# Gated mix of linear attention and a Mish layer: block 0 gives up two feature steps and takes its num products later, block 1 has an order of its own

## Chip, cores and metric

The kernel runs on one core of one Trainium2 chip. The metric is the device time of one execution in microseconds (us); lower is better. TensorE is PE in the profile, its weight loads PEld, VectorE is DVE, ScalarE is ACT, GpSimd is POOL, and SyncE, which issues nearly all DMAs, is SP.

## What is computed

```python
x = A_x                                        # (1, 2048, 512)
g = sigmoid((x * gate_w).sum(-1, keepdims=True))
q, k, v = split(x @ wqkv)                      # 32 heads of 16
pq = q @ w_phi; pk = k @ w_phi                 # per head, 16 x 16
phi = lambda p: concat([softmax(p), softmax(-p)])
kv = phi(pk).T @ v;  z = phi(pk).sum(rows)     # per head
o = (phi(pq) @ kv) / (phi(pq) @ z + 1e-6)
a = o @ wo
h = x @ w1 + b1                                # 512 -> 1376
b = mish(h) @ w2                               # 1376 -> 512
out = g * a + (1 - g) * b
```

All is fp32. Large products are made of three passes: each operand is split into a high part, rounded to the format that TensorE takes, and the rest (names with h and l), and high x high, high x low and low x high are added up.

## The kernel before

**Stage A** goes over the 2048 rows in 8 chunks of 256. It projects k and v, makes the features of k, adds up kv and z over all rows, and writes the projected q (pq) to DRAM (pqd). Weights are loaded and split along the way.

**Stage B** goes over the rows in four blocks of 512 (b = 0 to 3). A block has two threads of work that meet at its end.

- The Mish layer in 11 slices of 128 hidden units (i = 0 to 10). Each slice has `up` (12 matmuls, line 441), `mi` (Mish on ScalarE), `hi` (its high part, ScalarE), `lo` (the rest, GpSimd, line 461), and `down` (12 matmuls, line 465: three for each of the block's four row groups of 128, added up in four PSUM banks).
- The attention in four row groups of 128 (t = 0 to 3). `lq` loads pq. `mx`, `mn`, `d0`, `d1` (VectorE, lines 233 to 242) take the maximum and minimum per head away; `E` (ScalarE) is the exponential; `S`, `rS` (VectorE) the sums and their reciprocals; `T`, `D`, `m`, `de`, `rd`, `sc`, `es` (VectorE, lines 511 to 541 and 257) the denominator and the scaled features; `tr` (line 527) transposes blocks of 32 x 32 into the tile tt. For each half of a block (h = 0 for t = 0 and 1, h = 1 for t = 2 and 3), `mv` (line 546) moves tt into eT by 16 copies that SyncE issues, `nu` (line 552) multiplies eT with kv (16 matmuls, the num products), `oh` (ScalarE) and `ol` (VectorE) split the product into ohl, and `wo` (line 576, 12 matmuls per row group) multiplies it with wo. `ag` (ScalarE) scales by the gate, `fi` (VectorE, line 593) adds the gated Mish part and stores the rows.

Besides, `gr` takes the gate's logits out of one column of the first up product and brings them through DRAM into columns; `ge` and `gg` make the sigmoid of them. `LX`, `XH`, `XL` load and split x for the next block. `@z`, `@kt`, `WL` are leftovers of stage A in block 0.

**The order** is written out by hand. Each engine takes its instructions in the order in which the steps are named in a text: FIRST, STEADY, NEXT and LAST for stage A (lines 39 to 54), BLOCK0 for block 0 and BLOCK for the others (lines 58 to 74). `run` (line 187) calls the steps one after the other, and every instruction is pinned to that order. A name with `+` is the next block's step; a step that has run is not run again. So a block's first two row groups are worked on ahead, in the block before: in block 0, S1 is the first feature step left, since E0, E1 and S0 were made in LAST. In BLOCK0 and BLOCK, row groups 2 and 3 too are begun in the block before, up to their E (`mx2+` to `E3+`).

In `b_ops` (line 437), the down products of slices 0 to 8 are the steps `dn0` to `dn8`; those of slices 9 and 10 go by row group, as `df0` to `df3` of six matmuls each, each followed by its `fi`.

**What makes steps wait.** Tiles come from rings of few buffers. tt and eT have one buffer each: `tr2` and the next block's `tr0` wait until the copies of the half before have read tt, and `mv` waits until the num products before have read eT. PSUM has three banks with the tag "a" (up, the second half of num, every other wo), four for the down sums, and one with the tag "kv" (the first half of num, the other wo): `wo` of an even row group waits until the first half of `ol` has read the num product out of it. The tag "tx" (two buffers) holds T and the loaded x in turns, so `LX0` and `LX1` wait for the `D` of the next block's row groups 0 and 1. ScalarE has the exponential and Mish in different tables, and a change between them is a table load.

Of the kernel before, what the change touches and what calls it, by code (L numbers as in the profile page):

```python
# [30 lines left out]
NF = NFA + NFB  # L31
# [26 lines left out]
BLOCK0 = """  # L58
    up0 mi0 hi0 lo0 gr S1 rS1 mx2 mn2 d02 d12 up1 @z mi1 hi1 lo1 T0 D0 m0 de0 rd0 sc0 es0 tr0 up2 mi2 hi2 lo2 WL0 dn0
    T1 D1 m1 de1 rd1 sc1 es1 tr1 mv0 lq0+ lq1+ mx3 mn3 d03 d13 up3 @kt mi3 hi3 lo3 WL1 dn1  # L60
    up4 mi4 hi4 lo4 dn2 E2 E3 ge S2 T2 rS2 D2 m2 de2 rd2 sc2 es2 tr2 gg up5 mi5 hi5 lo5 dn3 up6 mi6 hi6 lo6 dn4 nu0 oh0 ol0
    S3 T3 rS3 D3 m3 de3 rd3 sc3 es3 tr3 mv1 up7 mi7 hi7 lo7 dn5 mx0+ mn0+ d00+ d10+ mx1+ mn1+ d01+ d11+ lq2+ lq3+
    up8 mi8 hi8 lo8 wo0 ag0 wo1 ag1 E0+ E1+ dn6 S0+ T0+ rS0+ D0+ m0+ de0+ rd0+ sc0+ es0+ tr0+
    up9 mi9 hi9 lo9 dn7 nu1 oh1 ol1 S1+ T1+ rS1+ D1+ LX0 LX1 m1+ de1+ rd1+ sc1+ es1+ tr1+ mv0+ up10 mi10 hi10 lo10 dn8
    mx2+ mn2+ d02+ d12+ mx3+ mn3+ d03+ d13+ XH0+ XL0+ XH1+ XL1+ wo2 ag2 wo3 ag3 E2+ E3+ df0 fi0 df1 fi1 df2 fi2 df3 fi3
"""
BLOCK = """
    up0 mi0 hi0 lo0 gr S2 T2 rS2 D2 m2 de2 rd2 sc2 es2 tr2 up1 mi1 hi1 lo1 up2 mi2 hi2 lo2 dn0 nu0 oh0 ol0
# [1 line left out]
    mx0+ mn0+ d00+ d10+ mx1+ mn1+ d01+ d11+ lq2+ lq3+ up5 mi5 hi5 lo5 dn3 E0+ E1+ ge gg wo0 ag0 wo1 ag1  # L70
    S0+ T0+ rS0+ D0+ m0+ de0+ rd0+ sc0+ es0+ tr0+ up6 mi6 hi6 lo6 dn4 nu1 oh1 ol1 S1+ T1+ rS1+ D1+ LX0 LX1 m1+ de1+ rd1+ sc1+
    es1+ tr1+ mv0+ up7 mi7 hi7 lo7 dn5 mx2+ mn2+ d02+ d12+ mx3+ mn3+ d03+ d13+ up8 mi8 hi8 lo8 dn6 E2+ E3+
    wo2 ag2 wo3 ag3 up9 mi9 hi9 lo9 dn7 up10 mi10 hi10 lo10 dn8 XH0+ XL0+ XH1+ XL1+ df0 fi0 df1 fi1 df2 fi2 df3 fi3
"""


# [1 line left out]
def tile_gated_mix(ctx: ExitStack, tc: tile.TileContext, xT, wv, wkT, wqT, bd, w1a, w1b, b1, w2a, w2b, wo, out):  # L78
# [9 lines left out]
    def mm(*a, **k):  # L88
        return pin(nc.tensor.matmul(*a, **k))  # L89
# [14 lines left out]
    def psum(name, tag, bufs={"a": 3, "dn": 4, "kv": 1}):  # L104
        nm[0] += 1
        return pp.tile([P, 512], F32, name=f"{name}_{nm[0]}", tag=tag, bufs=bufs[tag])
# [77 lines left out]
    def at(key, name, fn):  # L184
        steps.setdefault((key, name), []).append(fn)

    def run(text, key, prev=None, nxt=None):
        for w in text.split():
            k = prev if w.endswith("'") else nxt if w.endswith("+") else key
            for fn in steps.pop((k, w.rstrip("'+")), ()):  # L190
                fn()
# [160 lines left out]
    def w2_tile(f, x):  # L352
        n_, f = ("w2a", f) if f < NFA else ("w2b", f - NFA)
        return W[n_][0][x][:, f * 512 : (f + 1) * 512]
# [48 lines left out]
    B = {}  # L403
# [33 lines left out]
    def b_ops(b):  # L437
        key = ("B", b)
        U, dn, tts, eTs, num, ohl, io = {}, {}, {}, {}, {}, {}, {}

        def up(i):
            f = ORDER[i]
            xh, xl = xb[b]
            ps = psum("up", "a")
            n = 0
            for w, a in ((0, xh), (1, xh), (0, xl)):
                for k in range(KT):
                    mm(ps, w1_tile(f, w, k), a[:, k, :], start=(n == 0), stop=(n == 3 * KT - 1))
                    n += 1
            U[i] = {"ps": ps}  # L450

        def mi(i):
            f = ORDER[i]
            U[i]["a"] = k2("act", "hl")
            act(U[i]["a"], U[i]["ps"], AF.Mish, bias=b1s[:, f : f + 1])

        def hi(i):
            U[i]["h"] = k2("h", "hl", F32R)
            act(U[i]["h"], U[i]["a"])

        def lo(i):
            U[i]["l"] = k2("l", "hl", F32R)
            pin(G_.tensor_sub(U[i]["l"], U[i]["a"], f32(U[i]["h"])))  # L463

        def down(i, t):
            if t not in dn:
                dn[t] = psum("down", "dn")
            f = ORDER[i]
            h, l = [U[i][x][:, t * P : (t + 1) * P] for x in "hl"]
            for n, (a, x) in enumerate(((h, 0), (h, 1), (l, 0))):  # L470
                mm(dn[t], a, w2_tile(f, x), start=(i == 0 and n == 0), stop=(i == NF - 1 and n == 2))

        for i in range(NF):
            at(key, f"up{i}", lambda i=i: up(i))
            at(key, f"mi{i}", lambda i=i: mi(i))
            at(key, f"hi{i}", lambda i=i: hi(i))
            at(key, f"lo{i}", lambda i=i: lo(i))
            for t in range(4):
                at(key, f"dn{i}" if i < NF - 2 else f"df{t}", lambda i=i, t=t: down(i, t))


        cs = slice(4 * b, 4 * b + 4)
# [127 lines left out]
    for b in range(NB):  # L610
        b_ops(b)
# [51 lines left out]
    for c in range(1, NCH):  # L663
        run(STEADY if c < NCH - 2 else NEXT if c < NCH - 1 else LAST, ("A", c), ("A", c - 1), ("B", 0))
    for b in range(NB):
        run(BLOCK if b else BLOCK0, ("B", b), ("B", b - 1), ("B", b + 1))
    assert not steps, list(steps)


# [58 lines left out]
```

## Time and profile before

| what | value |
|---|---|
| runs | 475.44 us median of 3 (474.42 to 475.58) |
| the profiled execution: own time | 475.38 us |
| its span, first to last instruction | 473.6 us |
| busy: TensorE, VectorE, ScalarE, GpSimd | 462.3, 312.4, 194.0, 160.2 us |
| TensorE's mean granted clock | 0.991 of full speed |
| block 0, first up to the end of its last down | 161.46 to 245.02 us |

Times in the trace are microseconds from the span's start. A row of a time line has start, length (merged if xN is above 1), engine, line, operation, the tiles it writes and reads, and in square brackets the idle time just ahead of it on its engine with what ended it. The chain of waits follows the work that ended last back from the end; its rows have start, length and what. Rows of stretches (A:B) have, behind the length, the busy time of PE, PEld, DVE, ACT and POOL with instruction counts, then TensorE's granted clock, the DMA share and GB/s. Many lines are those of helpers: all matmuls have line 89, all ScalarE operations line 109, so tiles tell them apart.

### The profile page before, as it was taken

The page shows a single profiled execution, that of the slowest core. Times are in us where ns is not written, and L with a number is a line of the kernel's source. Part 1 is how long each engine was busy: PE and PEld are TensorE (multiplying, and loading weights), DVE is VectorE, ACT ScalarE, POOL GpSimd, SP SyncE. Part 2 cuts the span into 40 slices and gives each one's busy share as a digit, 9 for nine tenths or more (in the row PEclk, how much of TensorE's full clock was granted, in tenths as well). Part 3 has the DMA queues.
Part 4 walks back from the last instruction along what each step waited for, and adds up shares of the span by engine and source line. Part 5 has one row for each costly group of instructions (what it writes and reads, how often), then busy time and mean ns, then how long its engine had stood idle before and what let it go on. Part 6 is the DMA issues. An engine that isn't in the chain of part 4 may idle for free.

```text
span 473.6 us, 6002 instructions
## 1 busy us (share of the span) xinstructions
PE 462.3 (98%) x2292; PEld 375.4 (79%) x2292; DVE 312.4 (66%) x402; ACT 194.0 (41%) x263; POOL 160.2 (34%) x102
## 2 busy tenths in 40 slices
PE   7999999999999999699999999999999999999996
PEld 6888888888888878578787887887787888787885
DVE  2597648449498999888998967437867818621002
ACT  3544433533415644425455253533344452334221
POOL 3448685675861355211303212123111121321211
PEclk9999999999999999889999999999999999999999
DMA  7621531523514100403434141312041312020002
GB/s 289 222 89 46 177 101 57 174 62 122 181 42 157 44 2 1 124 10 88 133 85 140 36 142 46 88 44 91 2 117 59 101 33 91 1 72 18 0 2 89
DMA packets 25237, 40.01 MB, mean 84 GB/s; under 512 B 5620, under 2 KB 13812, under 8 KB 25208
## 3 DMA queue, kind: packets, MB, share of 16 engines
q1 hardware_dynamic: 25032, 39.35, 27.2%
q8 instruction: 18, 0.29, 0.3%
q10 hardware_dynamic: 144, 0.26, 0.2%
q14 instruction: 11, 0.09, 0.1%
q0 software_dynamic: 32, 0.01, 0.0%
HBM read 22.82 MB, written 8.40 MB: 66 GB/s over the span
## 4 chain that ended last, share of the span: by engine, by line
PE 86%; DVE 8%; SPq 2%; DMA 2%; POOL 1%; issue 1%; ACT 0%; POOLq 0%; DVEq 0%
PE proj L89 26%; PE down L89 22%; PE up L89 22%; PE wo L89 9%; PE num L89 4%; PE kvp L89 2%; SPq L550 2%; DMA wT<-in_wkT_dram 1%; PE fuse L89 1%; DVE E L257 1%; DVE Sm L246 1%; DVE Dn L537 1%; DVE E L240 1%; POOL zacc L295 1%; DVE E L242 1%
## 5 line engine op out<-in xcount | busy, mean ns | idle before, releaser
L463 POOL TENSOR_TENSOR l<-act,h 128x512 fp32r<-128x512 f32 x44 | 59.3, 1349 | 237.2 <-ACT h L109 208.5
L109 ACT ACTIVATE act<-up,b1s 128x512 f32<-128x512 f32 x44 | 30.3, 689 | 97.9 <-PE up L89 97.8
L295 POOL TENSOR_TENSOR zacc<-zacc,E 128x1024 f32<-128x1024 f32 x16 | 39.7, 2480 | 50.5 <-ACT v L109 37.3
L109 ACT ACTIVATE E<-E 128x1024 f32<-128x1024 f32 x32 | 33.5, 1058 | 42.7 <-DVE E L242 42.7
L257 DVE TENSOR_TENSOR E<-E,Sm 128x1024 f32<-128x1024 f32 x32 | 44.0, 1374 | 1.1
L89 PE MATMUL wo<-woh,ohl 128*128 128x512 f32 x128 | 40.7, 389 | 0.0
L246 DVE TENSOR_REDUCE Sm<-E 128x64 f32<-128x1024 f32 x32 | 38.7, 1210 | 2.2 <-ACT E L109 2.2
L89 PE MATMUL down<-w2ah,h 128*128 128x512 f32 x96 | 37.5, 390 | 0.0
L89 PE MATMUL down<-w2ah,l 128*128 128x512 f32 x96 | 37.4, 389 | 0.0
L89 PE MATMUL down<-w2al,h 128*128 128x512 f32 x96 | 37.3, 389 | 0.0
L233 DVE TENSOR_REDUCE mx<-proj 128x32 f32<-128x512 f32 x16 | 11.1, 691 | 37.3 <-PE proj L89 37.3
L595 DVE SCALAR_TENSOR_TENSOR io<-down,og_sb,io 128x512 f32<-128x512 f32 x16 | 11.5, 746 | 31.4 <-PE down L89 31.4
L89 PE MATMUL down<-w2bh,h 128*128 128x512 f32 x80 | 31.1, 389 | 0.0
L89 PE MATMUL down<-w2bl,h 128*128 128x512 f32 x80 | 31.1, 389 | 0.0
L89 PE MATMUL down<-w2bh,l 128*128 128x512 f32 x80 | 31.1, 389 | 0.0
L569 DVE TENSOR_TENSOR ohl<-num,ohl 128x512 fp32r<-128x512 f32 x16 | 10.9, 688 | 27.5 <-ACT ohl L109 27.5
L375 DVE TENSOR_TENSOR xbl<-xraw,xbh 128x1024 fp32r<-128x1024 f32 x8 | 12.2, 1566 | 24.7 <-ACT xbh L109 24.7
L109 ACT ACT_TABLE_LOAD x17 | 21.8, 1283 | 16.2 <-PE up L89 16.0
L109 ACT ACTIVATE h<-act 128x512 fp32r<-128x512 f32 x44 | 27.8, 632 | 1.5
L89 PEld LDWEIGHTS wo<-woh,ohl 128*128 128x128 f32 x128 | 24.0, 188 | 5.0
L89 PE MATMUL up<-xbh,w1ah 128*128 128x512 f32 x96 | 26.3, 396 | 0.2 <-ACT zb L109 0.2
L89 PE MATMUL up<-xbl,w1ah 128*128 128x512 f32 x96 | 25.7, 390 | 0.0
(113 smaller groups left out, 1019.7 us busy)
## 6 DMA issues: line engine op xcount, KB each, us to landing
xraw<-in_xT_dram SPq DMA_DIRECT2D x16, 512.0 KB, 3.5
eT<-tt SPq DMA_DIRECT2D x128, 64.0 KB, 2.0
pqd<-qs SPq DMA_DIRECT2D x16, 256.0 KB, 2.3
pq<-pqd SPq DMA_DIRECT2D x16, 256.0 KB, 2.9
out_dram<-io SPq DMA_DIRECT2D x16, 256.0 KB, 2.0
raw<-in_w1a_dram SPq DMA_DIRECT2D x3, 512.0 KB, 4.6
raw<-in_w2a_dram SPq DMA_DIRECT2D x3, 512.0 KB, 3.7
wT<-in_wkT_dram SPq DMA_DIRECT2D x4, 256.0 KB, 5.7
```

What stands on the lines that cost most here:

```text
L89: return pin(nc.tensor.matmul(*a, **k))
L109: return pin(A_.activation(out_, in_, fn, **k))
L233: pin(V.tensor_reduce(d[name], hv(src()), axis=AX.X, op=op))
L240: pin(V.tensor_sub(E, hv(src()), d["mx"][:, :, None].to_broadcast([P, H, DH])))
L246: pin(V.tensor_reduce(d["S"], hv(d["E"][:, :]), axis=AX.X, op=ALU.add))
L257: pin(eng.tensor_mul(hv(d["E"][:, :]), hv(d["E"][:, :]), d["S"][:, :, None].to_broadcast([P, 2 * H, DH])))
L295: at(key, f"z{t}", lambda d=d: pin(G_.tensor_add(zacc, zacc, d["E"])))
L375: pin(V.tensor_sub(xb[b][1][:, :, sl], kt(raw[h], SC), f32(xb[b][0][:, :, sl])))
L463: pin(G_.tensor_sub(U[i]["l"], U[i]["a"], f32(U[i]["h"])))
L550: pin(Sy.dma_start(eTs[h][32 * k : 32 * k + 32, :, q, :], tts[h][32 * q : 32 * q + 32, :, k, :]))
L569: pin(V.tensor_sub(ohl[h, gp][:, 512:], num[h, gp], f32(ohl[h, gp][:, :512])))
L595: pin(V.scalar_tensor_tensor(io[t], dn[t], og_sb[:, i : i + 1], io[t], op0=ALU.mult, op1=ALU.add))
```

## The change

Only the texts of the order and one name change; every instruction does what it did.

- BLOCK0: E3, ge and gg come later (E2 alone ahead of the slice up5, E3 behind dn3). nu0, oh0 and ol0 come behind up7 and dn5 instead of ahead of up7, with S3, T3, rS3 ahead of ol0. dn6 comes ahead of wo0. up10 and dn8 come ahead of nu1, and S1+, T1+, rS1+, D1+ ahead of ol1. The next block's mx2 to d13, E2 and E3 leave block 0.
- BLOCK1, new, for block 1: it begins with mx2 to d13 and, behind up1, E2 and E3, of its own row groups 2 and 3; up7 and dn5 come ahead of nu1. Else it is as BLOCK.
- In all blocks the down products of slice 9 are one step dn9 ahead of the df steps, which keep slice 10 alone, three matmuls each. In block 0 dn9 stands ahead of wo2, in the others behind dn8 (and XL1+).

```diff
 BLOCK0 = """
     up0 mi0 hi0 lo0 gr S1 rS1 mx2 mn2 d02 d12 up1 @z mi1 hi1 lo1 T0 D0 m0 de0 rd0 sc0 es0 tr0 up2 mi2 hi2 lo2 WL0 dn0
     T1 D1 m1 de1 rd1 sc1 es1 tr1 mv0 lq0+ lq1+ mx3 mn3 d03 d13 up3 @kt mi3 hi3 lo3 WL1 dn1
-    up4 mi4 hi4 lo4 dn2 E2 E3 ge S2 T2 rS2 D2 m2 de2 rd2 sc2 es2 tr2 gg up5 mi5 hi5 lo5 dn3 up6 mi6 hi6 lo6 dn4 nu0 oh0 ol0
-    S3 T3 rS3 D3 m3 de3 rd3 sc3 es3 tr3 mv1 up7 mi7 hi7 lo7 dn5 mx0+ mn0+ d00+ d10+ mx1+ mn1+ d01+ d11+ lq2+ lq3+
-    up8 mi8 hi8 lo8 wo0 ag0 wo1 ag1 E0+ E1+ dn6 S0+ T0+ rS0+ D0+ m0+ de0+ rd0+ sc0+ es0+ tr0+
-    up9 mi9 hi9 lo9 dn7 nu1 oh1 ol1 S1+ T1+ rS1+ D1+ LX0 LX1 m1+ de1+ rd1+ sc1+ es1+ tr1+ mv0+ up10 mi10 hi10 lo10 dn8
-    mx2+ mn2+ d02+ d12+ mx3+ mn3+ d03+ d13+ XH0+ XL0+ XH1+ XL1+ wo2 ag2 wo3 ag3 E2+ E3+ df0 fi0 df1 fi1 df2 fi2 df3 fi3
+    up4 mi4 hi4 lo4 dn2 E2 S2 T2 rS2 D2 m2 de2 rd2 sc2 es2 tr2 up5 mi5 hi5 lo5 dn3 E3 ge gg up6 mi6 hi6 lo6 dn4
+    up7 mi7 hi7 lo7 dn5 nu0 oh0 S3 T3 rS3 ol0 D3 m3 de3 rd3 sc3 es3 tr3 mv1 up8 mi8 hi8 lo8 dn6
+    mx0+ mn0+ d00+ d10+ mx1+ mn1+ d01+ d11+ lq2+ lq3+ wo0 ag0 wo1 ag1 E0+ E1+ S0+ T0+ rS0+ D0+ m0+ de0+ rd0+ sc0+ es0+ tr0+
+    up9 mi9 hi9 lo9 dn7 up10 mi10 hi10 lo10 dn8 S1+ T1+ rS1+ D1+ LX0 LX1 nu1 oh1 ol1 m1+ de1+ rd1+ sc1+ es1+ tr1+ mv0+
+    XH0+ XL0+ XH1+ XL1+ dn9 wo2 ag2 wo3 ag3 df0 fi0 df1 fi1 df2 fi2 df3 fi3
+"""
+BLOCK1 = """
+    up0 mi0 hi0 lo0 gr mx2 mn2 d02 d12 mx3 mn3 d03 d13 up1 mi1 hi1 lo1 E2 E3 S2 T2 rS2 D2 m2 de2 rd2 sc2 es2 tr2
+    up2 mi2 hi2 lo2 dn0 nu0 oh0 ol0 S3 T3 rS3 D3 m3 de3 rd3 sc3 es3 tr3 lq0+ lq1+ mv1 up3 mi3 hi3 lo3 dn1 up4 mi4 hi4 lo4 dn2
+    mx0+ mn0+ d00+ d10+ mx1+ mn1+ d01+ d11+ lq2+ lq3+ up5 mi5 hi5 lo5 dn3 E0+ E1+ ge gg wo0 ag0 wo1 ag1
+    S0+ T0+ rS0+ D0+ m0+ de0+ rd0+ sc0+ es0+ tr0+ up6 mi6 hi6 lo6 dn4 up7 mi7 hi7 lo7 dn5 nu1 oh1 ol1 S1+ T1+ rS1+ D1+ LX0 LX1
+    m1+ de1+ rd1+ sc1+ es1+ tr1+ mv0+ mx2+ mn2+ d02+ d12+ mx3+ mn3+ d03+ d13+ up8 mi8 hi8 lo8 dn6 E2+ E3+
+    wo2 ag2 wo3 ag3 up9 mi9 hi9 lo9 dn7 up10 mi10 hi10 lo10 dn8 XH0+ XL0+ XH1+ XL1+ dn9 df0 fi0 df1 fi1 df2 fi2 df3 fi3
 """
 BLOCK = """
...
-    wo2 ag2 wo3 ag3 up9 mi9 hi9 lo9 dn7 up10 mi10 hi10 lo10 dn8 XH0+ XL0+ XH1+ XL1+ df0 fi0 df1 fi1 df2 fi2 df3 fi3
+    wo2 ag2 wo3 ag3 up9 mi9 hi9 lo9 dn7 up10 mi10 hi10 lo10 dn8 XH0+ XL0+ XH1+ XL1+ dn9 df0 fi0 df1 fi1 df2 fi2 df3 fi3
...
-                at(key, f"dn{i}" if i < NF - 2 else f"df{t}", lambda i=i, t=t: down(i, t))
+                at(key, f"dn{i}" if i < NF - 1 else f"df{t}", lambda i=i, t=t: down(i, t))
...
-        run(BLOCK if b else BLOCK0, ("B", b), ("B", b - 1), ("B", b + 1))
+        run((BLOCK0, BLOCK1, BLOCK, BLOCK)[b], ("B", b), ("B", b - 1), ("B", b + 1))
```

## The prediction, made before the changed kernel had run

> **What bounds the kernel now.** I read the page's first part first, then the mean clock, then the chain of work that ended last, then the time lines of the engines around the one hole that they show.
>
> ```profile
> PE 462.3 (98%) x2292; PEld 375.4 (79%) x2292; DVE 312.4 (66%) x402; ACT 194.0 (41%) x263; POOL 160.2 (34%) x102
> ```
>
> ```profile
> core 0: 473.6 us, clock 0.991
> ```
>
> TensorE (PE) is busy for 462.3 us of a span of 473.6; the program's own time for this execution is 475.38 us, so 1.78 us lie outside the span. 11.3 us of idle TensorE are left, and a busy TensorE isn't always a fast one: a mean clock of 0.991 leaves 0.009 x 473.6 = 4.3 us of lost pulses. So whatever the change does, it can win some 3% at most, and only through holes. The chain of waits, read from 198 us on, shows the one hole inside the run:
>
> ```profile
> 198.11 2.00 DMA eT<-tt
> 200.11 0.04 issue
> 200.15 3.68 PE num L89 x16
> 203.83 3.73 PE up L89 x12
> ...
> 226.59 1.88 PE num L89 x16
> 228.47 2.94 PE up L89 x12
> 231.42 2.72 PE down L89 x12
> 234.14 5.44 PE wo L89 x24
> 239.58 5.44 PE down L89 x24
> ```
>
> The columns are start, length, what. The first num group of block 0 (step nu0) starts when the last copy eT<-tt has landed. It takes 3.68 us, and the up group after it 3.73; the same pair later, in the same block, takes 1.88 and 2.94. The last row, the closing down group of block 0, ends at 245.02: there block 1 starts. The time line of TensorE has the wait, and the stretches of 5 us have the clock:
>
> ```profile
> 200.15 3.68 PE L89 MATMUL num<-eT,kvb 128*64 128x256 f32 x16 [3.75 <-DMA eT<-tt]
> ```
>
> ```profile
> 195.00:200.00 5.00, 1.40 (x7) 0.82 (x5) 3.41 (x4) 0.72 (x2) 2.17 (x2) 0.87 0.43 102
> 200.00:205.00 5.00, 4.85 (x19) 2.76 (x20) 2.76 (x6) 1.19 (x2) 0.00 (x0) 0.50 0.31 104
> ```
>
> TensorE is free from 200.15 - 3.75 = 196.40, and after the wait its granted clock (third figure from the end) is 0.50 over 200 to 205. **The hole's price** is thus the wait, 3.75, and the slow clock, (3.68 - 1.88) + (3.73 - 2.94) = 1.80 + 0.79 = 2.59: together 6.34 us, 1.33% of 475.38.
>
> Why are the copies late? SyncE's time line:
>
> ```profile
> 188.36 10.34 SPq L550 DMA_DIRECT2D eT<-tt  x16
> 198.75 1.09 SPq L509 DMA_DIRECT2D pq<-pqd  x2
> 213.78 10.19 SPq L550 DMA_DIRECT2D eT<-tt  x16
> ```
>
> Sixteen copies take SyncE 10.2 to 10.3 us to issue, and the last lands 2.00 us after its issue. They can't start before tr1, the transpose of the second 128 rows, which ends on VectorE just before 188.36.
>
> **The change, part by part.**
>
> *nu0 behind up7 and dn5.* All steps up to E2 of block 0 stand as before on every engine, so the copies still land at 200.11. TensorE goes on at 196.40 with up7 (2.72) and dn5 (2.72): nu0 comes up at 201.84, 1.73 us after the landing. The wait goes, and with it the slow clock: **-6.34 us**. What is late next must be looked for down block 0. With the chain's prices (up after a num 2.94, a down or num after anything 2.72 or 1.88, wo 2.72 each) TensorE without a wait runs: nu0 201.84, up8 203.72, dn6 206.66, wo0 and wo1 209.38, up9 214.82, dn7 217.54, up10 220.26, dn8 222.98, nu1 225.70, dn9 227.58 (2.94, after a num), wo2 230.52, then wo3 and the four df (2.72 in all), block 1 at 238.68. I walk VectorE against that with these rows:
>
> ```profile
> 200.19 1.25 DVE L531 STREAM_TRANSPOSE tt<-E 128x1024 f32<-128x1024 f32 x1 [1.68 <-DMA eT<-tt]
> ...
> 201.73 0.17 DVE L496 TENSOR_SCALAR og_sb<-g_sb 128x4 f32<-128x4 f32 x1
> ...
> 209.36 1.16 DVE L521 SCALAR_TENSOR_TENSOR den<-Dn 128x32 f32<-128x32 f32 x1
> ...
> 221.57 1.22 DVE L246 TENSOR_REDUCE Sm<-E 128x64 f32<-128x1024 f32 x1 [2.17 <-ACT E L109]
> ...
> 229.06 1.25 DVE L569 TENSOR_TENSOR ohl<-num,ohl 128x512 fp32r<-128x512 f32 x2
> 230.24 1.20 DVE L246 TENSOR_REDUCE Sm<-E 128x64 f32<-128x1024 f32 x1
> ...
> 234.14 0.23 DVE L537 TENSOR_TENSOR Dn<-Dn,Sm 128x64 f32<-128x64 f32 x1
> 234.40 0.19 DVE L521 SCALAR_TENSOR_TENSOR den<-Dn 128x32 f32<-128x32 f32 x1
> ...
> 237.71 0.64 DVE L233 TENSOR_REDUCE mx<-pq 128x32 f32<-128x512 f32 x1
> ```
>
> A feature chain from S to tr lasts 229.06 - 221.57 = 7.49; its first four steps S, T, rS, D 234.14 - 230.24 = 3.90; a pair ol 1.18; mx, mn, d0 and d1 of two row groups are eight steps of at most 0.7, 5.6.
>
> *tr2 and gg* stay where the copies put them: tr2 waits for tt until 200.19 in both, gg ends at 201.90. The new place of lo5 on GpSimd, some 3 us earlier since E3 no longer stands ahead of mi5, may push S2's chain; that chain has 200.19 - 198.51 = 1.68 of idle (in the first row) as cover, so I cost it nothing. *S3, T3, rS3, ol0, D3 to tr3*: 201.90 + 7.49 + 1.18 = 210.57. ol0 is done at about 206, ahead of wo0 at 209.38. The copies mv1 then take 10.19 + 2.00, down at 222.8: nu1, put behind up10 and dn8, comes at 225.70. Margin 2.9.
>
> *The eight steps for block 1's first two row groups* end by 216.2, hidden: S0+ waits for E0+ on ScalarE, which waits for ag1:
>
> ```profile
> 218.47 0.69 ACT L109 ACTIVATE io<-wo,g_sb 128x512 f32<-128x512 f32 x1 [2.03 <-PE wo L89]
> 219.18 1.28 ACT L109 ACT_TABLE_LOAD   x1
> 220.47 2.01 ACT L109 ACTIVATE E<-E 128x1024 f32<-128x1024 f32 x2
> ```
>
> From ag1 at 218.47 to S at 221.57 are 3.10 us; ag1 moves to 214.85, S0+ to 217.95, and tr0+ ends at 225.44 (tt is free at 222.8). *S1+ to D1+ now stand ahead of ol1*: 225.44 + 3.90 = 229.34. The first half of ol1 is done at about 229.95, and wo2 needs it, at 230.52: margin 0.57, **the thinnest of all**. GpSimd can eat it:
>
> ```profile
> 209.14 1.33 POOL L463 TENSOR_TENSOR l<-act,h 128x512 fp32r<-128x512 f32 x1 [11.97 <-ACT h L109]
> ```
>
> While this lo ran, VectorE's den step took 1.16 instead of 0.19 (209.36 against 234.40): 0.97 lost. Two lo (of up9 and up10) fall into 217.95 to 229.34. I take one hit: ol1's half at 230.92, **wo2 waits 0.40**; the bounds are 0 (no hit) and 1.4 (two hits). The Trainium skill has a rule for it, "SBUF — State Buffer", on the shared port pair: a VectorE operation with two SBUF inputs and a GpSimd operation that reads SBUF hold the pair by turns for a whole instruction, and the later one blocks. By it, two hits at the very start of a lo would cost 2 x 1.33 = 2.7 and the wait would be 2.1 (an estimate); the row above, with a finish at 210.52 after a GpSimd end at 210.47, agrees. That is the first rival below.
>
> *Features 2 and 3 of block 1 at that block's head.* XL0+ and XL1+ follow tr1+ directly, which ends at 229.34 + 0.97 + 1.18 + (7.49 - 3.90) = 235.1; two steps as wide as tr2's 1.25, they are done by 237.6, ahead of block 1 (239.08 with the 0.40). The eight steps run behind fi3, to about 246. E2 waits on ScalarE for mi1 and hi1, behind up1's end at 244.5:
>
> ```profile
> L109 ACT ACTIVATE act<-up,b1s 128x512 f32<-128x512 f32 x44 | 30.3, 689 | 97.9 <-PE up L89 97.8
> ```
>
> Two steps of 0.7, a table load of 1.28 and an E of 1.0 put S2 at about 248.5. Its chain, ol0 and S3's chain end near 264.7 (7.49 + 1.18 + 7.49), two pq loads (1.09) and the copies (12.2) are down at 278; nu1 of block 1, put behind up7 and dn5, stands at 249.96 + 1.88 + 2.94 + 11 x 2.72 = 284.7. Margin 6.7: nothing. nu0 of block 1 reads copies that start at 235.1 and land at 247.3; TensorE is there at 249.96 (four groups of 2.72 after 239.08). Margin 2.7: nothing. If either cover were gone, each microsecond behind it costs one. Two more table loads on ScalarE (E3 apart from E2) stand beside TensorE's up and down groups: nothing.
>
> *dn9 ahead of the df steps, in all blocks.* The same twelve matmuls. The last three stores of the run come 0.68 apart instead of 1.36. The stores of block 0, issued half a microsecond apart, and the last four land so (first block 0, then the run's end):
>
> ```profile
> DMA to landing us min/median/max: 2.4/2.5/2.7
> ```
>
> ```profile
> DMA to landing us min/median/max: 2.0/2.0/2.0
> ```
>
> So the end is later by 0 to 0.7; between the two rows I take **+0.3**.
>
> **Sum.** -6.34 + 0.40 + 0.3 = -5.6 against this execution's 475.38: 469.8 us, ahead of the runs' median of 475.44 by 1.2%. Bounds of the terms: -6.34 + 0 + 0 and -6.34 + 2.1 + 0.7, that is 469.0 to 471.8.
>
> **The rivals.**
>
> *ol1 late.* Both lo hit, and wo2 waits 1.4 to 2.1: 475.38 - 6.34 + 1.75 + 0.3 = 471.1. For it: the thin margin, and the row of 1.16. Against: D and S are reductions, and den's neighbours (0.23, 0.19) are short, so a lo has to fall on a small part of the chain. Whether so short a wait also slows the clock is bounded by nothing and by 2.59. On that the Trainium skill, "TensorE: Matmul & The Clock Gate", says that the clock halves after an idle window of about 3.4 us; by it 1.4 to 2.1 us cost themselves alone, and the row of 3.75 with its 0.50 agrees.
>
> *The wait moves to nu1 of block 0.* Its copies need tr3 and 12.2 us of copying. If VectorE ran 6 us behind the walk there, nu1 would wait 3.1 plus up to 2.59 and all would be as before, 475.4. Against: the walk up to tr3 has one lo in it, 0.97 of 2.9.
>
> *Slower, at nu0 of block 1.* The place is the VectorE queue from S0+ to tr1+, behind which its copies stand; SyncE also holds them behind the load LX1, which waits for D1+. The margin is 2.7. A slip of 7.2 us makes a wait of 4.5 plus 2.59, 7.1 against the 5.64 gained: from there the kernel is slower by more than can be measured. With a slip of 8: 475.38 - 5.64 + 5.3 + 2.59 = 477.6. For it: all the margins hang on this one queue, and SyncE issues in order. Against: two lo give 1.9 to 2.7, and no row shown reaches 7.
>
> **How the numbers follow.** Forecast (wo2 waits at most 1 us): 0.76. ol1 late: 0.15. Wait at nu1: 0.03. Slower at block 1: 0.06. A difference under 0.3%, 1.4 us, couldn't be told from none. Faster is forecast and first rival, 0.91; same 0.03; slower 0.06. The range takes the terms' bounds and the runs' own spread (474.42 to 475.58, as much as 1.0 below this execution's time and 0.2 above): 468.4 to 472.0.
>
> **What would show it.** In the changed profile: the num group of block 0 without a wait, 1.88 long, near 201.8; a clock of 1.00 over 200 to 205; block 1's first up near 239 instead of 245.02; the second num near 225.7 without a wait; a wait of up to 1 us for VectorE's ohl ahead of wo2; the rest of the run moved as a whole by some 6 us; the last store landing 2.0 to 2.7 us after its issue. The prediction is wrong if a num group still waits for eT, if wo2 waits over 2 us, or if the clock shows another 0.50.

## The result, and the profile after

The changed kernel takes 470.51 us (median of 4 runs, 469.57 to 470.98) against 475.44 (4 runs, 474.42 to 475.58): a ratio of 0.9898, 95% interval 0.9886 to 0.9909. It is faster by 1.0%; 469.8 was forecast.

The profiled execution took 469.57 us. Its span and mean clock:

```profile
core 0: 467.9 us, clock 1.000
```

The time line of TensorE has no wait at a num group any more; the first one, and the stretches around it, now read:

```profile
201.65 1.95 PE L97 MATMUL num<-eT,kvb 128*64 128x256 f32 x16
```

```profile
195.00:200.00 5.00, 5.00 (x24) 4.14 (x23) 2.16 (x5) 2.13 (x4) 2.02 (x1) 1.00 0.42 100
200.00:205.00 5.00, 5.00 (x30) 3.40 (x29) 4.87 (x8) 1.65 (x3) 1.29 (x1) 1.00 0.32 104
```

(Lines are 8 higher than before: 97 for 89.) TensorE is busy in the whole of both stretches, where it was for 1.40 us of the first, and the clock is 1.00 instead of 0.50 in the second. The only new wait of TensorE stands ahead of wo2 of block 0, for ol1:

```profile
230.74 0.50 PE L97 MATMUL wo<-woh,ohl 128*128 128x512 f32 x1 [0.34 <-DVE ohl L577]
```

In the chain of waits that place and what follows it read:

```profile
230.74 5.74 PE wo L97 x24
236.48 2.72 PE down L97 x12
239.20 8.16 PE up L97 x36
247.36 2.72 PE down L97 x12
250.08 1.88 PE num L97 x16
```

The two wo groups take 5.74 us behind the wait, against 5.44 without one, so ol1 costs 0.34 + 0.30 = 0.64. The 0.30 is no second wait, since TensorE shows no idle time inside the groups. It goes with the restart: without a wait a group begins 0.16 before the one ahead of it has ended (in e5_ol1_earlier below, wo begins at 231.65 and the dn9 ahead of it ends at 231.81), and behind the wait the second matmul starts 0.34 after the first, where 0.23 is usual. Block 1 starts at 239.20 instead of 245.02, and its num products (250.08) don't wait.

**The opening moves.** The profiles differ in when block 0 begins. Two of them, the changed kernel and a later one (e5_again below):

```profile
161.35 1.20 PE L97 MATMUL up<-xbh,w1ah 128*128 128x512 f32 x4
```

```profile
163.55 1.20 PE L97 MATMUL up<-xbh,w1ah 128*128 128x512 f32 x4
```

These 2.2 us come before anything that any of these kernels changes, and the kernel before alone begins block 0 at 161.46, 161.87 and 162.88 in its three profiled executions. So I compare spans from block 0's first up to the end, and name this **the rest**: before 473.6 - 161.46 = 312.1, the changed kernel 467.9 - 161.35 = 306.6 (306.55).

### The profile page after: what moved, and what is told of

The parts are those of the page before. It is cut to its first block, busy times and chain, and to the rows that moved or that the text cites. A ratio compares the mean times of both kernels' runs of the same rounds, so it can differ in the third digit from the quotient of the medians.

```text
span 467.9 us, 6005 instructions
## 1 busy us (share of the span) xinstructions
PE 460.0 (98%) x2292; PEld 374.0 (80%) x2292; DVE 310.6 (66%) x402; ACT 196.4 (42%) x265; POOL 161.7 (35%) x102
## 4 chain that ended last, share of the span: by engine, by line
PE 91%; DVE 3%; SPq 2%; DMA 2%; issue 0%; ACT 0%; DVEq 0%
PE proj L97 28%; PE up L97 24%; PE down L97 23%; PE wo L97 8%; PE kvp L97 3%; PE num L97 3%; SPq L558 2%; DMA wT<-in_wkT_dram 1%; PE fuse L97 1%; DMA pq<-pqd 1%; DVE tt L539 1%; DVE Dn L525 0%; DVE io L603 0%; DVE ohl L577 0%; DVE Sm L533 0%
## 5 line engine op out<-in xcount | busy, mean ns | idle before, releaser
L471 POOL TENSOR_TENSOR l<-act,h 128x512 fp32r<-128x512 f32 x44 | 61.0, 1385 | 229.9 <-ACT h L117 207.0
L97 PE MATMUL up<-xbh,w1al 128*128 128x512 f32 x96 | 25.7, 389 | 0.0
```

## The experiments

Theory: the gain is the hole at nu0, a wait and a slow clock, and the other parts of the change keep new holes from opening behind it. Rivals: that the work taken off VectorE in block 0 is the gain in itself; that nu0's move is all of it; that dn9 is a small cost.

The ratios are to runs of the kernel before that were taken beside each kernel, with medians of 475.44, 475.45, 475.53 and 475.16 us.

| kernel | median us (runs) | ratio to before, 95% | span | first up | rest |
|---|---|---|---|---|---|
| before | 475.44 (4) | | 473.6 | 161.46 | 312.1 |
| changed | 470.51 (4) | 0.9898 (0.9886 to 0.9909) | 467.9 | 161.35 | 306.6 |
| e1_nu0_only | 476.55 (6) | 1.0025 (1.0013 to 1.0037) | 475.8 | 162.30 | 313.5 |
| e2_nu0_back | 476.29 (10) | 1.0015 (1.0005 to 1.0024) | 474.5 | 161.59 | 312.9 |
| e3_nu0_after_up7 | 471.07 (4) | 0.9908 (0.9892 to 0.9925) | 469.2 | 161.61 | 307.6 |
| e4_nu0_half_dn5 | 472.36 (10) | 0.9948 (0.9929 to 0.9966) | 470.6 | 161.62 | 309.0 |
| after_again | 470.68 (4) | 0.9899 (0.9886 to 0.9911) | 468.5 | 161.94 | 306.6 |
| e5_ol1_earlier | 470.28 (4) | 0.9891 (0.9877 to 0.9905) | 468.6 | 162.76 | 305.8 |
| e7_after_no_dn9 | 475.11 (12) | 0.9979 (0.9961 to 0.9996) | 474.2 | 163.43 | 310.8 |
| e8_feats_in_block0 | 471.14 (4) | 0.9913 (0.9901 to 0.9926) | 470.3 | 162.64 | 307.7 |
| e5_again | 470.07 (6) | 0.9897 (0.9876 to 0.9918) | 469.4 | 163.55 | 305.9 |

**nu0's move alone.**

```diff
 (BLOCK0 of before)
-    ... up6 mi6 hi6 lo6 dn4 nu0 oh0 ol0
-    S3 T3 rS3 D3 m3 de3 rd3 sc3 es3 tr3 mv1 up7 mi7 hi7 lo7 dn5 mx0+ ...
+    ... up6 mi6 hi6 lo6 dn4
+    up7 mi7 hi7 lo7 dn5 nu0 oh0 ol0 S3 T3 rS3 D3 m3 de3 rd3 sc3 es3 tr3 mv1 mx0+ ...
```

> Only nu0, oh0 and ol0 go behind up7 and dn5; everything else is the kernel before (nu1 ahead of up10, features 2 and 3 of the next block in block 0, no dn9). If the wait at nu0 were all that matters, it goes with its slow clock, -6.3 us: 469.1. The rival, walked with the rows of before: S3's chain now starts behind ol0, tr3 ends near 213, the copies for nu1 land at 225.3, and TensorE, which is now early, comes to nu1 near 220.3: a new wait of 5 us there, and 2.6 us of slow clock after it: 475.4 - 6.3 + 5.1 + 2.6 = 476.8.

476.55: slower than before, as the walk had it. The first num group is without a wait (202.57), and the second has a worse one:

```profile
225.84 3.68 PE L89 MATMUL num<-eT,kvb 128*64 128x256 f32 x16 [4.77 <-DMA eT<-tt]
```

```profile
225.00:230.00 5.00, 4.16 (x17) 2.41 (x18) 2.65 (x3) 1.04 (x2) 0.00 (x0) 0.50 0.69 213
```

The wait moved from nu0 to nu1, with its half clock: the num group takes 3.68 again, and the up group behind it 4.02. "All that matters is nu0" falls.

**All but nu0's move.**

```diff
 (BLOCK0 of the changed kernel)
-    ... up6 mi6 hi6 lo6 dn4
-    up7 mi7 hi7 lo7 dn5 nu0 oh0 S3 T3 rS3 ol0 ...
+    ... up6 mi6 hi6 lo6 dn4 nu0 oh0
+    up7 mi7 hi7 lo7 dn5 S3 T3 rS3 ol0 ...
```

> The changed kernel with nu0 and oh0 back ahead of up7; all other parts of the change stay. If the gain is the hole at nu0, the wait of 3.75 us and the slow clock of 2.6 come back: 470.5 + 6.3 = 476.8, about the kernel before. The rival, that less work on VectorE in block 0 brings the gain, leaves it near 471.

476.29, and the old hole:

```profile
200.26 3.68 PE L97 MATMUL num<-eT,kvb 128*64 128x256 f32 x16 [3.74 <-DMA eT<-tt]
```

VectorE's relief brings nothing while the wait at nu0 stays. The kernel is even slower than before by 0.15%, with ol1's wait on top (0.34 there too).

**Shorter waits at nu0.** e3 puts nu0 and oh0 between up7 and dn5; e4 puts them behind half of dn5:

```diff
 (e3)
-    up7 mi7 hi7 lo7 dn5 nu0 oh0 S3 ...
+    up7 mi7 hi7 lo7 nu0 oh0 dn5 S3 ...
 (e4; da5 and db5 are dn5 for row groups 0, 1 and 2, 3)
-    ... lo6 dn4
-    up7 mi7 hi7 lo7 dn5 nu0 oh0 S3 ...
+    ... lo6 dn4 da5
+    nu0 oh0 db5 up7 mi7 hi7 lo7 S3 ...
```

> The changed kernel with nu0 and oh0 between up7 and dn5: TensorE comes to nu0 at about 199.1, the copies land at 200.1, a wait of 1.0 us. If the slow clock needs a wait of some 3.4 us or more, the price is the wait alone: 471.5 and a granted clock of 1.00 behind it. If any wait of this kind halves the clock, it is 1.0 + 2.6 more: 474.1.

> The changed kernel with half of dn5 (two row groups, 1.36 us), then nu0 and oh0, then the rest of dn5 and up7: a wait of about 2.4 us. If the slow clock needs some 3.4 us: 470.5 + 2.4 = 472.9, clock 1.00. If it halves the clock: 475.5.

The first num group in e3 and in e4, and the stretch behind it in e4:

```profile
200.29 1.95 PE L97 MATMUL num<-eT,kvb 128*64 128x256 f32 x16 [1.02 <-DMA eT<-tt]
```

```profile
200.30 1.95 PE L97 MATMUL num<-eT,kvb 128*64 128x256 f32 x16 [2.38 <-DMA eT<-tt]
```

```profile
200.00:205.00 5.00, 4.70 (x28) 3.42 (x29) 4.59 (x8) 1.20 (x2) 0.00 (x0) 1.00 0.31 108
```

In these two executions the wait costs itself alone: the rest is 307.6 (+1.0) and 309.0 (+2.4) against 306.6, and the clock is 1.00. Of e4's ten runs, eight lie at 471.99 to 472.74 and two at 475.18 and 475.83, with a mean clock of 0.996 and 0.995. These two have no profile. A halved clock behind the wait would explain part of the 3 us (at most 1.7, by the lengths of the half clock given further below), but one run of e5_again, a kernel whose profiled execution has no such wait, was at 472.12 with 0.993, so that stays open.

**dn9 taken out.**

```diff
-at(key, f"dn{i}" if i < NF - 1 else f"df{t}", ...)
+at(key, f"dn{i}" if i < NF - 2 else f"df{t}", ...)      # and dn9 out of the texts
```

> The changed kernel with the down products of slice 9 in the df steps again, as before. The prediction charged dn9 with a cost of 0 to 0.7 us at the run's end, so without it 470.2. The rival: dn9 is what covers ol1, since TensorE now comes from nu1 straight to wo2 at 227.6 and ol1's first half is done at 230.6: a wait of 3.1 us at wo2, and if that halves the clock up to 2.6 more: 473.3 to 475.9.

475.11: nearly the whole gain is gone, and the wait sits at wo2. The chain of waits, the time line and the stretch behind it:

```profile
232.84 7.34 PE wo L97 x24
```

```profile
232.84 0.50 PE L97 MATMUL wo<-woh,ohl 128*128 128x512 f32 x1 [3.29 <-DVE ohl L577]
```

```profile
235.00:240.00 5.00, 5.00 (x19) 4.05 (x18) 4.13 (x4) 1.75 (x2) 0.00 (x0) 0.80 0.18 43
```

The wo pair takes 7.34 instead of 5.44: 1.90, of which 0.30 stood behind the short wait of the changed kernel too, and 1.60 goes with the slow clock. The rival holds: dn9 is the cover of ol1. The twelve runs fall into two groups: four at 472.44 to 472.60 with a mean clock of 1.00, eight at 474.72 to 475.99 with 0.992 to 0.996. By the mean clock, then, it halves in some executions of one and the same kernel and not in others. A second profile was to tell whether that sets the group:

> The changed kernel without dn9, once more: its runs fell into two groups, four near 472.5 with a mean clock of 1.00 and eight from 474.7 to 476.0 with 0.992 to 0.996. If the group is set by whether the wait of 3.3 us at wo2 halves the clock, a run near 472.5 shows 1.00 behind the wait and 307.2 + 2.2 = 309 us or so from block 0's first up to the end, and one near 475 a stretch of 0.5 to 0.9 behind it and about 311.

It took 474.89, with the same wait of 3.29 and the slow stretch right behind it; the rest is 473.2 - 162.45 = 310.8, as in the first:

```profile
230.00:235.00 5.00, 3.14 (x7) 2.48 (x8) 4.83 (x10) 1.11 (x2) 0.00 (x0) 0.66 0.30 108
```

No profile shows the group at 472.5; that its clock stayed whole is read from its mean of 1.00 alone, and that it had the same wait is assumed. The slow clock's 1.6 is also less than the 2.8 us between the groups. The two profiled executions began block 0 late (163.43 and 162.45), which may be the rest; that stays open.

**Features 2 and 3 back in block 0.**

```diff
 (BLOCK0 of the changed kernel; block 1 takes BLOCK)
-    XH0+ XL0+ XH1+ XL1+ dn9 wo2 ag2 wo3 ag3 df0 ...
+    mx2+ mn2+ d02+ d12+ mx3+ mn3+ d03+ d13+ XH0+ XL0+ XH1+ XL1+ dn9 wo2 ag2 wo3 ag3 E2+ E3+ df0 ...
```

> The changed BLOCK0 with mx2+ to d13+ put back ahead of XH0+ and E2+, E3+ back ahead of df0, and BLOCK for block 1: the work on VectorE in block 0 is that of before, the num products stay late. If only the num products matter: 470.5. The rival, that VectorE's work has to leave block 0: eight steps of 0.6 us put XL0+ and XL1+ past block 1's start at 239.1, and its first up waits about 1.9 us: 472.4.

471.14; the rest is 307.7, 1.1 more than the changed kernel's. The wait is in block 1's first up, though not at its head: the first matmuls that read xbl are its third part, 1.8 us on. There it is 0.88 long, where 1.9 had been expected at the head:

```profile
243.21 1.19 PE L89 MATMUL up<-xbl,w1ah 128*128 128x512 f32 x4 [0.88 <-DVE xbl L375]
```

By the profiles the work moved out of block 0 is worth about 1 us; the runs' medians differ by 0.5 to 0.6, and their intervals overlap. Either way most of the gain stays without it.

**ol1 two steps earlier**, beside the changed kernel once more:

```diff
-    ... dn8 S1+ T1+ rS1+ D1+ LX0 LX1 nu1 oh1 ol1 m1+ ...
+    ... dn8 S1+ T1+ nu1 oh1 ol1 rS1+ D1+ LX0 LX1 m1+ ...
```

> The changed kernel once more, beside the three that follow: 470.5, and a wait of 0.3 us at wo2 of block 0.

> The changed kernel with nu1, oh1 and ol1 ahead of rS1+ and D1+ on VectorE (and the loads LX0, LX1 behind ol1), nothing else on TensorE. The walk with the rows gives ol1's first half at about 228.6 to 229.2, 1.2 us ahead of wo2: the wait of 0.34 us at wo2 goes, 470.2; LX1 moves back by 1.2 us and is covered. The rival, that the wait comes from the matmuls' order (dn9 to wo2) and not from ol1, leaves the 0.34 in the trace.

> The changed kernel with ol1 ahead of rS1+, once more: 305.9 us from block 0's first up to the end, against 306.6 of the changed kernel, with no wait at wo2 and 5.44 instead of 5.74 for the two wo groups; 470.2 in the runs, the difference of 0.7 hardly seen over the scatter of the opening.

The wait at wo2 is gone in both profiles; the chain of the first:

```profile
228.87 2.94 PE down L97 x12
231.81 5.44 PE wo L97 x24
237.25 2.72 PE down L97 x12
```

The rest is 305.8 and 305.9 against 306.6 twice: 0.7 less, of which 0.34 + 0.30 are the wait and the wo pair. By the runs (470.28 and 470.07 against 470.51 and 470.68) it is the best version, but their intervals overlap: the opening scatters by more.

**The price of the slow clock before.** The kernel before was profiled twice more.

> The kernel before, profiled once more. Open: most of its runs have a mean clock of 0.996 and some 0.991, with nearly the same time. If the slow clock behind nu0's wait has one price, the num and up groups of block 0 take 3.68 and 3.73 again and the time from block 0's first up to the span's end is 312.1 us. If its price varies from run to run, the pair is shorter by up to 1.9 us at 0.996.

> As the run ahead of it: 312.1 us from block 0's first up to the end if the slow clock has one price, up to 1.9 us less if it varies; the first up itself between 161.3 and 163.5, as in the profiles so far.

They took 475.90 and 474.63, with a mean clock of 0.996. The same wait of 3.75 stands ahead of nu0 in both, but the pair behind it is shorter; first again, then third:

```profile
201.57 3.49 PE num L89 x16
205.06 3.04 PE up L89 x12
```

```profile
200.55 3.34 PE num L89 x16
203.89 2.94 PE up L89 x12
```

Against 1.88 and 2.94 that is 1.71 and 1.46 us lost, not 2.59, and the rest is 474.2 - 162.88 = 311.3 and 472.9 - 161.87 = 311.0, not 312.1. The price does vary.

Stretches of half a microsecond show why. First the two in which the clock drops and comes back in the execution that the prediction read (before), then in the second one (before_again):

```profile
198.50:199.00 0.50, 0.00 (x0) 0.00 (x0) 0.01 (x1) 0.00 (x0) 0.00 (x0) 0.66 0.46 111
205.00:205.50 0.50, 0.50 (x2) 0.40 (x2) 0.50 (x2) 0.00 (x0) 0.00 (x0) 0.52 0.00 0
```

```profile
201.50:202.00 0.50, 0.43 (x4) 0.34 (x6) 0.40 (x1) 0.00 (x0) 0.00 (x0) 0.80 0.47 94
205.00:205.50 0.50, 0.50 (x4) 0.46 (x3) 0.00 (x0) 0.40 (x1) 0.00 (x0) 0.79 0.00 0
```

Between the two rows of a pair the clock is 0.50, and outside them 1.00. A row's mean tells where in it the change lies, so the clock is halved from 198.66 to 205.48 in the first and from 201.80 to 205.21 in the second. That is 6.8 and 3.4 us, and every half clock in these profiles has one of these two lengths: 3.4 in before_again, before_third and both profiles of e7, 6.8 in before, e1 and e2. Its start isn't tied to the wait. In before the clock drops 2.3 us after TensorE stopped, while it still waits; in before_again it drops 0.2 us after nu0 has begun. What is lost is about half of the slow stretch in which TensorE works: (205.48 - 200.15) / 2 = 2.67 in before, 2.59 by its groups; (205.21 - 201.80) / 2 = 1.71 in before_again, 1.71 by its groups.

Of the 49 further runs of the kernel before that list their mean clock, 33 have 0.996, which is what one half clock of 3.4 us takes off it (an estimate: 1 - 3.4 / 2 / 474), and 14 have 0.991 or 0.993. One has 1.000, and at 473.60 us it is the fastest of them. So the prediction's price came from the rarer kind of execution.

## Why the prediction was right, point by point

*The hole at nu0* was the cause: e2 puts it back and the gain is gone. TensorE came to nu0 at 201.7 (201.84 forecast), behind the copies. Like for like, between the profiled execution that the sum started from and that of the changed kernel, the rest fell by 312.1 - 306.6 = 5.6 us, as summed (5.64). That the sum is met so closely is in part luck: ol1 cost 0.24 more than its term of 0.40, and dn9 about 0.2 less than its term of 0.3, as told below.

*The term that was mis-sized* is the slow clock's 2.59. It was read from one execution, and the two other profiles of before have 1.71 and 1.46. With these the sum is about 0.9 to 1.1 smaller, -4.5 to -4.8, and the runs' medians moved by 4.93. This, more than any step of the walk, is why 470.5 was measured where 469.8 was forecast. The opening has a part in it too: the execution that the sum started from had the earliest first up of the three of before (161.46), so that its dear clock didn't show in its time, and the changed kernel's profiled execution, with an opening as early, took 469.57. The range held both. Its lower end is a slip, though: 469.0 less 1.0 is 468.0, not 468.4.

*wo2's wait for ol1* was 0.34, 0.40 forecast, and the mechanism is in the rows: one lo hit the m step of VectorE's chain, and not den.

```profile
221.55 1.28 POOL L471 TENSOR_TENSOR l<-act,h 128x512 fp32r<-128x512 f32 x1 [12.14 <-ACT h L117]
```

```profile
221.77 1.15 DVE L545 TENSOR_TENSOR Dn<-Dn,Sm 128x64 f32<-128x64 f32 x1
222.95 0.19 DVE L529 SCALAR_TENSOR_TENSOR den<-Dn 128x32 f32<-128x32 f32 x1
...
231.20 0.22 DVE L545 TENSOR_TENSOR Dn<-Dn,Sm 128x64 f32<-128x64 f32 x1
```

The step that takes 0.22 at 231.20 takes 1.15 here and ends at 222.92, just behind lo's end at 222.83. That is what the Trainium skill, "SBUF — State Buffer", section "Who interferes with whom", says of the shared port pair: of a VectorE instruction with two SBUF inputs and a GpSimd instruction that reads SBUF, the second to start blocks until the first has finished. VectorE has no idle time from 217.84 to ol1, so without this hit ol1's half would have been there 0.9 earlier, ahead of TensorE. The prediction left out the 0.30 of the restart behind the wait.

*The margin at nu1* was given as 2.9 and was about 1.2: two more lo, not counted there, took 0.5 from gg and 1.1 from sc of row group 3, and the copies started at 212.11, not 210.57. Their landing at 224.3 was still ahead of nu1 at 225.5.

*Block 1* went as walked: its start at 239.20 (239.08 forecast), S2 at 248.50 (248.5), nu0 at 250.08 (249.96), nu1 at 284.82 (284.7). The rival that would have made it slower had no part.

*dn9* was priced as a cost at the end of the run, 0 to 0.7. Little of it is there: from block 1's first up to the end the changed kernel takes 467.9 - 239.20 = 228.7 and the kernel before 473.6 - 245.02 = 228.6. The last four stores landed in

```profile
DMA to landing us min/median/max: 2.0/2.1/2.1
```

As an edit it was misjudged all the same: the walk had dn9 in TensorE's line, but the text didn't say that it covers ol1, and without it 4.2 us of the rest come back. In the same way the prediction put the whole gain at nu0's move, while that move alone (e1) makes the kernel slower. Its conditions lie in what the changed kernel has beside it. With the features back in block 0 (e8) most of the gain stays, so the two features' leaving isn't one of them. The other parts, among them the later nu1, dn9 and the later E3, ge and gg, were added together; only dn9 was taken out alone, so the share of the others isn't shown. The sum was right because the walk held all of them.

## What to carry to other kernels

A wait on an engine that is always busy is worth itself plus what it does to the clock, but moving the waiting step helps only if every later consumer of the same slow chain is moved along: walk the whole block with both queues side by side and write down each margin. An edit that looks like mere reordering (dn9) can be the cover that the rest lives on, so take it out once to see. Price a clock effect from several executions, look at where in each the slow stretch begins and ends, and compare spans from a point behind the opening's scatter.

## What the runs showed of the hardware that wasn't expected

One and the same wait doesn't always have the same effect on TensorE's clock. At 3.75 us three profiles show 1.46, 1.71 and 2.59 us lost; at 3.29 both profiles show a slow stretch, while four of twelve runs have a mean clock of 1.00 and are about 2.8 us faster than the others; at 2.38 and 1.02 the profiles show none. The half clock lasts 3.4 or 6.8 us, and TensorE need not have been idle for 3.4 us when it begins: in before it begins 2.3 us after TensorE stopped. So the length of a wait alone doesn't tell whether the clock halves, nor for how long. The Trainium skill, "TensorE: Matmul & The Clock Gate", section "Part 1: The HAM clock gate", speaks of a window of about 3.4 us that runs free of the kernel. The two lengths, and a price that depends on where the wait falls, agree with that. The Trainium skill has the clock halve there after at least one idle window; a wait of 3.29, and 2.3 us without work in before, are below the figure, and the measurement decides.
